# Last block of two chained MLPs: three subtractions on another engine, the two accumulators stored in the other order, stores issued by two queues

## The chip, the cores and the metric

The kernel runs on one core of one Trainium2 chip. The metric is the device time of one execution in microseconds (us); the median of several runs is what counts. The engines are TensorE (PE, matrix products; its weight loads are PEld), VectorE (DVE), ScalarE (ACT), GpSimd (POOL) and SyncE (SP, which here only issues DMAs). In lists of waits, PEq, ACTq and SPq are the instruction queues of engines.

## The reference

Only what matters is kept. A causal convolution over 7 positions with one set of softmax weights for each of 8 groups of channels gives 16384 tokens of 192 channels; two MLPs with 2048 hidden channels follow one another.

```python
def _attn_ref(x, weight):            # x: 4 x 4096 x 192, weight: 8 x 7
    w = softmax(weight, axis=-1)
    ...
    out = np.einsum('hk,bskhg->bshg', w, x_unf)     # 7 shifted copies of x
    return out.reshape(B, S, D).astype(np.float32)

def _moe_ref(x, w_in, w_out):        # w_in: 192 x 2048, w_out: 2048 x 192
    h = x @ w_in
    g = h * np.cos(h)
    return (g @ w_out).astype(np.float32)

def _moe2_ref(x, w_in, w_out):
    h = x @ w_in
    g = np.where(h > 0.0, h, np.exp(np.minimum(h, 0.0)) - 1.0)
    return (g @ w_out).astype(np.float32)
```

## The kernel before

The tokens are cut into 32 blocks of 512, kept with the channels on the partitions. Each hidden layer is cut into 16 pieces of 128 channels, so that one step is (m, b, f): MLP m (1 or 2), block b, piece f. There are 1024 steps in the list `steps` (m = 1 and m = 2 alternate by groups of four blocks), and `total` is their number. The last sixteen steps are MLP 2 of block 31, the last block.

Products are made of numbers split in a high and a low part (`gh` and `gl`, `wo_h` and `wo_l`), both in the type fp32r, so that a sum of several products keeps nearly the precision of float32. Of one step s, `emit_A` makes five products of 512 columns into the PSUM tile `u` (L474). ACT and DVE work out the activation into `w` (for MLP 2: L484, L501 on ACT, then L509 on DVE). `emit_hi` rounds `w` to `gh` on ACT (L515), and `emit_lo` makes the low part `gl = w - gh` on POOL (L520). `emit_B` adds five products to the block's two accumulators `a[0]` and `a[1]` (L531 to L535): three with `gh`, two with `gl`. `a[0]` holds the output channels 0 to 127. `a[1]` holds the last 64 channels in two halves of its partitions, which still have to be added.

`step(s)` sets the order: A of step s, then `emit_act2` and `emit_g` of step s-1, `emit_hi` and `emit_lo` of step s-2 (HID = 2) and B of step s-5 (LAG = 5). So when the last A is done, six Bs are left for PE: those of the steps total-6 to total-1. There are three buffers for `gh` and two for `gl` (`bufs=3`, `bufs=2`): a `gl` may be written only when the B two steps earlier has read its buffer.

After B of a block's last piece, `evac` empties the accumulators. For m = 1 it makes the four tiles that MLP 2 reads (L544 to L549). For m = 2 it queues the generator `store(b, a)`: ACT copies the upper half of `a[1]` (L563), DVE transposes `a[0]` in blocks of 32 x 32 (L565), SP issues four stores of 32 channels each, 64 KB (L560); then DVE adds the two halves of `a[1]` (L568) and transposes the sum (L571), and SP issues two more stores. For block 31 all of this comes after the last product.

The order of all instructions on an engine is the order of the code, with one exception. The first 108 steps (`for s in range(FREE)`) stand outside `tc.manual_schedule()`: there a scheduler at build time orders the instructions of each engine by its own estimates of times. In these steps DVE, ACT and POOL also split the weights of both MLPs (the function `decode`, L176 to L184, works on pieces of `raw`), and DVE applies the convolution (L355, L357).

Of the kernel before, what the change touches and what calls it, by code (L numbers as in the profile page):

```python
# [9 lines left out]
F32 = mybir.dt.float32  # L10
# [4 lines left out]
ALU = mybir.AluOpType  # L15
AX = mybir.AxisListType

P = 128
N = 512
Q = 32  # L20
# [16 lines left out]
def conv_then_two_mlps(ctx, tc, x, weight, w_in1, w_out1, w_in2, w_out2, out):  # L37
# [9 lines left out]
    nc = tc.nc  # L47
# [8 lines left out]
    D2 = D - P  # L56
    HALO = K - 1
    NBLK = T // N
# [7 lines left out]
    op = ctx.enter_context(tc.tile_pool(name="op", bufs=1))  # L66
# [10 lines left out]
    f32 = lambda ap: ap.bitcast(F32)  # L77
# [3 lines left out]
    oseg = out.rearrange("(i j) d -> i j d", j=J)  # L81
# [381 lines left out]
    wrk = {}  # L463
# [47 lines left out]
    gs = {}  # L511
# [5 lines left out]

    def emit_lo(s):
        gl = wk.tile([P, N], F32R, tag="gl", name="gl", bufs=2)
        nc.gpsimd.tensor_tensor(out=gl, in0=wrk.pop(s), in1=f32(gs[s][0]), op=ALU.subtract)  # L520
        gs[s].append(gl)

    def emit_B(s):
        m, b, f = steps[s]
        gh, gl = gs.pop(s)
        st, sp = f == 0, f == NF - 1
        if f == 0:
            acc[m, b] = [ps_a.tile([P, N], F32, tag="acc", name="acc") for _ in range(2)]
        a = acc[m, b]
        h, l, sel = (wo[m, n] for n in ("h", "l", "s"))  # L530
        nc.tensor.matmul(a[0], lhsT=l[:, f, :], rhs=gh, start=st, stop=False)  # L531
        nc.tensor.matmul(a[0], lhsT=h[:, f, :], rhs=gh, start=False, stop=False)  # L532
        nc.tensor.matmul(a[1], lhsT=sel[:, f, :], rhs=gh, start=st, stop=False)  # L533
        nc.tensor.matmul(a[0], lhsT=h[:, f, :], rhs=gl, start=False, stop=sp)  # L534
        nc.tensor.matmul(a[1], lhsT=sel[:, f, :], rhs=gl, start=False, stop=sp)  # L535
        if f == NF - 1:
            evac(m, b)

    def evac(m, b):
        a = acc.pop((m, b))  # L540
        if m == 1:
            xh, xl, x3, x4 = (zt.tile([P, N], F32R, tag=n, name=n) for n in ("zh", "zl", "z3", "z4"))
            al = op.tile([P, N], F32R, tag="al", name="al")[0:D2]
            nc.scalar.activation(out=xh, in_=a[0], func=AF.Copy, scale=TWO_PI)  # L544
            nc.scalar.activation(out=x4, in_=a[1], func=AF.Copy, scale=TWO_PI)
            nc.vector.scalar_tensor_tensor(out=xl, in0=a[0], scalar=TWO_PI, in1=f32(xh), op0=ALU.mult, op1=ALU.subtract)
            nc.vector.scalar_tensor_tensor(out=al, in0=a[1][0:D2], scalar=TWO_PI, in1=f32(x4[0:D2]), op0=ALU.mult, op1=ALU.subtract)
            nc.sync.dma_start(out=f32(x3[0:D2]), in_=f32(x4[0:D2]))
            nc.sync.dma_start(out=f32(x3[D2:P]), in_=f32(al))  # L549
            xs[2, b] = (xh, xl, x3, x4)  # L550
        else:
            chores.append(store(b, a))

    def store(b, a):
        cols = lambda ap: ap.rearrange("p (j i) -> p j i", i=Q)
        j = slice(b * JB, (b + 1) * JB)

        def put(o, ch0, n):
            for ch in range(0, n, Q):
                nc.sync.dma_start(out=oseg[:, j, ch0 + ch:ch0 + ch + Q], in_=cols(o[ch:ch + Q]))  # L560

        lower = op.tile([P, N], F32, tag="al", name="lower")[0:D2]
        nc.scalar.activation(out=lower, in_=a[1][D2:P], func=AF.Copy)  # L563
        o = op.tile([P, N], F32, tag="o1", name="o")
        nc.vector.transpose(out=o, in_=a[0])  # L565
        put(o, 0, P)
        yield
        nc.vector.tensor_tensor(out=lower, in0=a[1][0:D2], in1=lower, op=ALU.add)  # L568
        yield
        o = op.tile([P, N], F32, tag="o2", name="o")  # L570
        nc.vector.transpose(out=o[0:D2], in_=lower)  # L571
        put(o, P, D2)
        yield
# [102 lines left out]
    def emit_B2(s):  # L676
        need("out", steps[s][0], steps[s][2])
        emit_B(s)

    def step(s):  # L680
# [21 lines left out]
        if 0 <= s - HID < total:  # L702
            emit_lo(s - HID)
# [14 lines left out]
    total = len(steps)  # L718
# [56 lines left out]
```

## Time and profile before

| | us |
|---|---|
| median of 3 runs | 2382.76 |
| lowest and highest of these | 2382.19, 2385.02 |
| the profiled execution, its own time | 2383.45 |
| its span, first to last instruction | 2381.7 |
| PE busy in the span | 2357.3 (99%) |
| ACT, DVE, POOL busy | 1890.7, 1548.2, 1414.3 |

The span is read from the trace, and the execution's own time lies 1.75 us above it. A busy PE is the sum over overlapping products; the trace shows a product of 512 columns as 0.39 us long, while one starts every 0.227 us. A share of busy time says little about the two ends of the program, where an engine that is idle on average can be what everything waits for.

### The profile page before, as it was taken

To read this page: it belongs to the slowest core of one execution; us is meant where nothing else is said; L and a number is where in the kernel's file an instruction comes from. 1 tells how busy PE (TensorE), PEld (TensorE's weight loads), DVE (VectorE), ACT (ScalarE), POOL (GpSimd) and SP (SyncE) were. 2 spreads that over 40 slices of the span, in tenths; PEclk is the share of its full clock that TensorE was granted. 3 is DMA by queue.
4 is the path that set the end of the run, shared out by engine and by line. 5 is a ranking of instruction groups with operands and counts; after the bars stand their busy time and mean duration, and the time that the engine had idled before them with its cause. 6 is when DMAs were issued, how large, how long until landed. Compare 5 with 4: busy or idle time off the path is not lost.

```text
span 2381.7 us, 32340 instructions
## 1 busy us (share of the span) xinstructions
PE 2357.3 (99%) x10354; PEld 1936.5 (81%) x10354; DVE 1548.2 (65%) x2292; ACT 1890.7 (79%) x3378; POOL 1414.3 (59%) x1144
## 2 busy tenths in 40 slices
PE   8899999999999999999999999999999999999998
PEld 5678888888888888888888888888888888888887
DVE  6997569943699337983379733896349963497433
ACT  7888787787877878777787878778787787877876
POOL 6888655555555555555555555555555555555555
PEclk9999999999999999999999999999999999999999
DMA  6123111100111002110011001110011100110000
GB/s 167 47 71 81 26 24 28 30 10 10 29 29 25 12 7 34 27 22 12 14 28 37 16 7 17 26 37 16 7 20 33 26 16 14 18 19 16 5 14 14
DMA packets 251116, 65.05 MB, mean 27 GB/s; under 512 B 226112, under 2 KB 239424, under 8 KB 250944
## 3 DMA queue, kind: packets, MB, share of 16 engines
q1 hardware_dynamic: 250496, 62.59, 13.8%
q8 instruction: 81, 1.33, 0.2%
q14 instruction: 91, 0.75, 0.1%
q10 hardware_dynamic: 448, 0.39, 0.1%
HBM read 29.91 MB, written 12.58 MB: 18 GB/s over the span
## 4 chain that ended last, share of the span: by engine, by line
PE 95%; DVE 3%; ACT 1%; DMA 1%; issue 0%; ACTq 0%; SPq 0%; POOL 0%; DVEq 0%
PE u L474 47%; PE acc L531 9%; PE acc L533 9%; PE acc L532 9%; PE acc L534 9%; PE acc L535 9%; DVE y L357 1%; DVE w L493 1%; DVE w L507 1%; PE y L400 0%; DMA early<-in_moe_w_in_dram 0%; DVE w L181 0%; DVE early L182 0%; DVE t L180 0%; ACT w L482 0%
## 5 line engine op out<-in xcount | busy, mean ns | idle before, releaser
L520 POOL TENSOR_TENSOR gl<-w,gh 128x512 fp32r<-128x512 f32 x1024 | 1336.6, 1306 | 928.2 <-PE acc L535 595.8
L509 DVE SCALAR_TENSOR_TENSOR w<-w,u 128x512 f32<-128x512 f32 x512 | 351.7, 687 | 675.1 <-ACT w L501 654.6
L515 ACT ACTIVATE gh<-w 128x512 fp32r<-128x512 f32 x1024 | 643.7, 629 | 20.8 <-DVE w L507 8.3
L499 ACT ACTIVATE w<-w 128x512 f32<-128x512 f32 x512 | 323.1, 631 | 203.6 <-DVE w L493 199.5
L484 ACT ACTIVATE w<-u 128x512 f32<-128x512 f32 x512 | 306.6, 599 | 211.9 <-PE u L474 208.3
L474 PE MATMUL u<-xh,wi_hl 128*128 128x512 f32 x1024 | 399.4, 392 | 12.9 <-DVE w L507 6.5
L507 DVE TENSOR_TENSOR w<-u,w 128x512 f32<-128x512 f32 x512 | 348.9, 682 | 88.1 <-ACT w L499 83.5
L531 PE MATMUL acc<-gh,wo_l 128*128 128x512 f32 x1024 | 399.6, 390 | 1.9 <-ACT gh L515 1.9
L534 PE MATMUL acc<-gl,wo_h 128*128 128x512 f32 x1024 | 399.6, 390 | 0.8 <-POOL gl L520 0.6
L535 PE MATMUL acc<-gl,wo_s 128*128 128x512 f32 x1024 | 398.4, 389 | 0.0
L533 PE MATMUL acc<-gh,wo_s 128*128 128x512 f32 x1024 | 398.4, 389 | 0.0
L532 PE MATMUL acc<-gh,wo_h 128*128 128x512 f32 x1024 | 398.4, 389 | 0.0
L474 PE MATMUL u<-zh,wi_hl 128*128 128x512 f32 x1024 | 397.7, 389 | 0.0
L493 DVE SCALAR_TENSOR_TENSOR w<-u,w 128x512 f32<-128x512 f32 x512 | 347.6, 679 | 10.8 <-ACT w L482 9.4
L501 ACT ACTIVATE w<-w 128x512 f32<-128x512 f32 x512 | 317.0, 619 | 0.6
L482 ACT ACTIVATE w<-u 128x512 int32<-128x512 f32 x512 | 299.2, 585 | 22.2 <-PE u L474 19.2
L474 PE MATMUL u<-x,wi_s 128*128 128x512 f32 x1024 | 315.8, 390 | 0.0
L474 PE MATMUL u<-z,wi_s 128*128 128x512 f32 x1024 | 315.2, 389 | 0.0
L357 DVE SCALAR_TENSOR_TENSOR y<-xT,wch,y 128x512 f32<-128x512 f32 x276 | 297.5, 1078 | 0.2
L474 PEld LDWEIGHTS u<-xh,wi_hl 128*128 128x128 f32 x1024 | 192.5, 188 | 59.3 <-DVE w L507 10.8
L531 PEld LDWEIGHTS acc<-gh,wo_l 128*128 128x128 f32 x1024 | 192.2, 188 | 43.6 <-ACT gh L515 3.4
L534 PEld LDWEIGHTS acc<-gl,wo_h 128*128 128x128 f32 x1024 | 192.1, 188 | 43.7 <-POOL gl L520 4.1
(94 smaller groups left out, 2352.8 us busy)
## 6 DMA issues: line engine op xcount, KB each, us to landing
out_dram<-o SPq DMA_DIRECT2D x192, 64.0 KB, 2.0
xa<-in_x_dram SPq DMA_DIRECT2D x112, 88.0 KB, 3.0
xc<-in_x_dram SPq DMA_DIRECT2D x56, 88.0 KB, 3.0
z<-z SPq DMA_DIRECT2D x32, 128.0 KB, 2.3
z<-al SPq DMA_DIRECT2D x32, 128.0 KB, 2.2
x<-ch SPq DMA_DIRECT2D x30, 128.0 KB, 2.2
x<-cl SPq DMA_DIRECT2D x30, 128.0 KB, 2.3
early<-in_moe_w_out_dram SPq DMA_DIRECT2D x12, 256.0 KB, 4.3
```

Of the source, the lines that this page charges most:

```text
L474: led[0] = nc.tensor.matmul(u, lhsT=wi[m, w][:, c], rhs=xx, start=i == 0, stop=i == len(ops) - 1).ins
L493: paced[0] = nc.vector.scalar_tensor_tensor(out=w, in0=u, scalar=0.25, in1=w.bitcast(I32), op0=ALU.add, op1=ALU.subtract).ins
L499: nc.scalar.activation(out=w, in_=w, func=AF.Sin, scale=6.283185)
L507: nc.vector.tensor_tensor(out=w, in0=u, in1=w, op=ALU.mult)
L509: paced[0] = nc.vector.scalar_tensor_tensor(out=w, in0=w, scalar=-1.0, in1=u, op0=ALU.add, op1=ALU.max).ins
L515: nc.scalar.activation(out=gh, in_=wrk[s], func=AF.Copy)
L520: nc.gpsimd.tensor_tensor(out=gl, in0=wrk.pop(s), in1=f32(gs[s][0]), op=ALU.subtract)
L531: nc.tensor.matmul(a[0], lhsT=l[:, f, :], rhs=gh, start=st, stop=False)
L532: nc.tensor.matmul(a[0], lhsT=h[:, f, :], rhs=gh, start=False, stop=False)
L533: nc.tensor.matmul(a[1], lhsT=sel[:, f, :], rhs=gh, start=st, stop=False)
L534: nc.tensor.matmul(a[0], lhsT=h[:, f, :], rhs=gl, start=False, stop=sp)
L535: nc.tensor.matmul(a[1], lhsT=sel[:, f, :], rhs=gl, start=False, stop=sp)
```

## The change

In the last three steps (total-3, total-2, total-1) the subtraction of `emit_lo` runs on DVE in place of POOL. In `emit_B`, in all steps, the product of `gl` with `wo_s` into `a[1]` comes ahead of the product of `gl` with `wo_h` into `a[0]`, so that `a[1]` is finished first. For the last block alone, `store` adds and transposes `a[1]` first, issues its two stores, and only then transposes `a[0]` and issues four. Of these six stores SP issues three and ACT three.

```diff
     def emit_lo(s):
         gl = wk.tile([P, N], F32R, tag="gl", name="gl", bufs=2)
-        nc.gpsimd.tensor_tensor(out=gl, in0=wrk.pop(s), in1=f32(gs[s][0]), op=ALU.subtract)
+
+        engine = nc.vector if s >= total - 3 else nc.gpsimd
+        engine.tensor_tensor(out=gl, in0=wrk.pop(s), in1=f32(gs[s][0]), op=ALU.subtract)
         gs[s].append(gl)
...
         nc.tensor.matmul(a[1], lhsT=sel[:, f, :], rhs=gh, start=st, stop=False)
+        nc.tensor.matmul(a[1], lhsT=sel[:, f, :], rhs=gl, start=False, stop=sp)
         nc.tensor.matmul(a[0], lhsT=h[:, f, :], rhs=gl, start=False, stop=sp)
-        nc.tensor.matmul(a[1], lhsT=sel[:, f, :], rhs=gl, start=False, stop=sp)
         if f == NF - 1:
             evac(m, b)
...
         def put(o, ch0, n):
             for ch in range(0, n, Q):
-                nc.sync.dma_start(out=oseg[:, j, ch0 + ch:ch0 + ch + Q], in_=cols(o[ch:ch + Q]))
-
+
+                queue = nc.scalar if b == NBLK - 1 and ch // Q % 2 else nc.sync
+                queue.dma_start(out=oseg[:, j, ch0 + ch:ch0 + ch + Q], in_=cols(o[ch:ch + Q]))
+
+        last = b == NBLK - 1
         lower = op.tile([P, N], F32, tag="al", name="lower")[0:D2]
         nc.scalar.activation(out=lower, in_=a[1][D2:P], func=AF.Copy)
+        if last:
+
+            nc.vector.tensor_tensor(out=lower, in0=a[1][0:D2], in1=lower, op=ALU.add)
+            o2 = op.tile([P, N], F32, tag="o2", name="o")
+            nc.vector.transpose(out=o2[0:D2], in_=lower)
+            put(o2, P, D2)
         o = op.tile([P, N], F32, tag="o1", name="o")
         nc.vector.transpose(out=o, in_=a[0])
         put(o, 0, P)
+        if last:
+            return
         yield
```

With it the lines move: in the new code POOL's subtraction is L522, the five products of B are L533 to L537, the stores are issued at L564, and the last block's chain is L568, L571, L573, L576.

DVE at the end of the program, before. The rows begin in the store of block 30; L509 is the activation of a step of MLP 2.

```order
L565 STREAM_TRANSPOSE o<-acc 128x512
L509 SCALAR_TENSOR_TENSOR w<-w,u 128x512
L568 TENSOR_TENSOR lower<-acc,lower 64x512
L509 SCALAR_TENSOR_TENSOR w<-w,u 128x512
L571 STREAM_TRANSPOSE o<-lower 64x512
L509 SCALAR_TENSOR_TENSOR w<-w,u 128x512 x10
L565 STREAM_TRANSPOSE o<-acc 128x512
L568 TENSOR_TENSOR lower<-acc,lower 64x512
L571 STREAM_TRANSPOSE o<-lower 64x512
```

DVE at the same place, after:

```order
L509 SCALAR_TENSOR_TENSOR w<-w,u 128x512 x9
L522 TENSOR_TENSOR gl<-w,gh 128x512
L509 SCALAR_TENSOR_TENSOR w<-w,u 128x512
L522 TENSOR_TENSOR gl<-w,gh 128x512 x2
L571 TENSOR_TENSOR lower<-acc,lower 64x512
L573 STREAM_TRANSPOSE o<-lower 64x512
L576 STREAM_TRANSPOSE o<-acc 128x512
```

One subtraction now stands ahead of the last activation (L509 of step total-1), two behind it, and the transposition of `a[0]` has gone from the first to the last place of the final three.

ACT at the end of the program, after; before, the rows were the same up to the copy `lower<-acc` (L563), and that was the last.

```order
L484 ACTIVATE w<-u 128x512
L515 ACTIVATE gh<-w 128x512
L501 ACTIVATE w<-w 128x512
L515 ACTIVATE gh<-w 128x512 x2
L568 ACTIVATE lower<-acc 64x512
L564 DMA out_dram<-o 32x16x32 x3
```

ACT now issues three stores behind its copy, and SP's last row of stores has 21 in place of 24.

DVE in the first 108 steps, where the scheduler puts the order together: the piece of the difference around the second block's hand-over from MLP 1 to MLP 2. L546 and L547 before (L548 and L549 after) empty the accumulators, L507 and L493 belong to activations of MLP 1, L178 to L182 split weights, L445 splits a block of input.

```order
-L546 SCALAR_TENSOR_TENSOR zl<-acc,zh 128x512
-L547 SCALAR_TENSOR_TENSOR al<-acc,z_1365 64x512
-L507 TENSOR_TENSOR w<-u,w 128x512
-L445 TENSOR_TENSOR xl<-y,xh 128x512
-L178 TENSOR_SCALAR t<-raw 128x256
+L549 SCALAR_TENSOR_TENSOR al<-acc,z_1365 64x512
+L548 SCALAR_TENSOR_TENSOR zl<-acc,zh 128x512
+L507 TENSOR_TENSOR w<-u,w 128x512
+L445 TENSOR_TENSOR xl<-y,xh 128x512
 L493 SCALAR_TENSOR_TENSOR w<-u,w 128x512 x2
```

The two that empty the accumulators have changed places, since `a[1]` is now finished first, and from here on the splitting of weights is dealt out differently among the activations. Ahead of the first such swap the order of DVE, ACT and POOL is what it was; with the last of the 108 steps the difference ends.

## Rows read from the trace of the kernel before

**Rows 1.** Busy time by stretch (us from the start), PEclk is the granted clock:

```profile
core 0: us, PE busy (x) PEld busy (x) DVE busy (x) ACT busy (x) POOL busy (x), PEclk, DMA share, GB/s
10.00:20.00 10.00, 5.42 (x22) 2.55 (x22) 6.92 (x15) 5.00 (x15) 3.79 (x7) 1.00 1.09 303
60.00:110.00 50.00, 42.67 (x171) 30.16 (x170) 48.02 (x84) 39.42 (x84) 41.63 (x39) 1.00 0.17 40
110.00:130.00 20.00, 20.00 (x89) 16.17 (x88) 18.80 (x27) 16.21 (x31) 13.60 (x12) 1.00 0.21 49
130.00:140.00 10.00, 8.85 (x39) 6.79 (x38) 8.49 (x17) 7.81 (x17) 5.95 (x5) 1.00 0.26 78
140.00:160.00 20.00, 20.00 (x90) 16.52 (x89) 18.90 (x41) 18.22 (x39) 19.07 (x21) 1.00 0.33 86
160.00:2360.00 2200.00, 2200.00 (x9708) 1821.67 (x9707) 1408.15 (x2029) 1756.09 (x3094) 1286.76 (x1003) 1.00 0.12 22
```

**Rows 2.** Timeline of the end: start, duration, [idle before <- releaser]:

```profile
2369.37 5.05 POOL L520 TENSOR_TENSOR gl<-w,gh 128x512 fp32r<-128x512 f32 x4 [0.97 <-PE acc L535]
2370.04 0.69 DVE L509 SCALAR_TENSOR_TENSOR w<-w,u 128x512 f32<-128x512 f32 x1 [1.58 <-ACT w L501]
...
2371.32 0.40 PE L531 MATMUL acc<-gh,wo_l 128*128 128x512 f32 x1
2371.38 0.63 ACT L515 ACTIVATE gh<-w 128x512 fp32r<-128x512 f32 x1 [0.78 <-PE acc L533]
...
2371.98 0.19 PEld L534 LDWEIGHTS acc<-gl,wo_h 128*128 128x128 f32 x1 [0.24 <-POOL gl L520]
...
2373.23 0.19 PEld L534 LDWEIGHTS acc<-gl,wo_h 128*128 128x128 f32 x1 [0.26 <-POOL gl L520]
...
2374.47 0.19 PEld L534 LDWEIGHTS acc<-gl,wo_h 128*128 128x128 f32 x1 [0.25 <-POOL gl L520]
...
2374.82 0.39 PE L535 MATMUL acc<-gl,wo_s 128*128 128x512 f32 x1
2375.01 0.72 DVE L565 STREAM_TRANSPOSE o<-acc 128x512 f32<-128x512 f32 x1 [4.29 <-PE acc L534]
2375.24 0.59 ACT L563 ACTIVATE lower<-acc 64x512 f32<-64x512 f32 x1 [3.23 <-PE acc L535]
2375.76 3.04 SPq L560 DMA_DIRECT2D out_dram<-o  x6
2375.87 0.68 DVE L568 TENSOR_TENSOR lower<-acc,lower 64x512 f32<-64x512 f32 x1
2376.59 0.70 DVE L571 STREAM_TRANSPOSE o<-lower 64x512 f32<-64x512 f32 x1
```

**Rows 3.** Chain that ended last: five products without a wait, then the last three Bs:

```profile
2366.93 1.13 PE u L474 x5
...
2371.25 0.23 PE acc L535
2371.48 0.23 PE acc L531
...
2374.98 0.24 PE acc L535
2375.22 0.02 issue
```

**Rows 4.** The last six stores: durations of the issues, last issue, time to landing:

```profile
L560 SPq DMA_DIRECT2D out_dram<-o x6: 315/494/507, 2375.8 to 2378.3; - x6
DMA to landing us min/median/max: 1.8/2.0/2.0
2378.30 0.51 SPq L560 DMA_DIRECT2D out_dram<-o  x1
```

**Rows 5.** DMA engines from 2376.6 to 2379.95: busy tenths, then packets and share:

```profile
DMA  4899885799885899988579989568989757999961
q1 hardware_dynamic: 3167, 0.39, 80.8%
```

**Rows 6.** Two queues issuing side by side at the start of the program:

```profile
1.28 3.86 SPq L283 DMA_DIRECT2D rows<-in_x_dram  x4
0.82 1.19 ACTq L209 DMA_DIRECT2D early<-in_moe_w_in_dram  x2
2.05 1.28 ACTq L194 DMA_DIRECT2D early<-in_moe_w_in_dram  x2
```

**Rows 7.** A DVE subtraction of two SBUF tiles: ns min/median/max, 32 of them:

```profile
L445 DVE TENSOR_TENSOR xl<-y,xh x32: 671/1137/1458, 20.8 to 2177.2; 128x512 fp32r<-128x512 f32 x32
```

**Rows 8.** Groups of DVE by line and shape: busy us, mean ns:

```profile
L507 DVE TENSOR_TENSOR w<-u,w 128x512 f32<-128x512 f32 x512 | 348.9, 682 | 88.1 <-ACT w L499 83.5
L493 DVE SCALAR_TENSOR_TENSOR w<-u,w 128x512 f32<-128x512 f32 x512 | 347.6, 679 | 10.8 <-ACT w L482 9.4 <-POOL w L184 0.7
L180 DVE TENSOR_SCALAR t<-t 128x256 f32<-128x256 f32 x46 | 19.6, 427 | 9.8 <-ACT t L179 9.6
```

**Rows 9.** The chain that ended last, around 130 us:

```profile
128.94 1.46 DVE y L357
130.40 0.02 issue
130.42 3.16 DMA raw<-in_moe_w_out_dram
```

## The prediction

> **What bounds the kernel now.** I read the busy times by stretch first, then the end of the timeline, then the stores. From 160 to 2360 us PE is busy for all of 2200 us at a granted clock of 1.00, and the list of who waits for whom has nothing for PE in between [rows 1]. Nothing in that stretch gets shorter unless PE has fewer products, and the change removes none. What can move is the two ends: the first 140 us, where PE lost 7.33 us between 60 and 110 and 1.15 us between 130 and 140 [rows 1], and the end, from the last six Bs to the last instruction at 2381.7.
>
> The end before, event by event. POOL makes the last four `gl` back to back, 5.05 us for 4, that is 1.26 each [rows 2], while a B takes PE only 5 x 0.227 = 1.13. So each of the last three Bs waits a little for its `gl`: their weight loads stood idle 0.24, 0.26 and 0.25 us [rows 2]. On the chain, these three Bs run from 2371.48 to 2375.22, 3.74 us, where 15 products at 0.227 (1.13 for five) take 3.40 [rows 3]: 0.34 us lost. The last product ends at 2374.82 + 0.39 = 2375.21. DVE transposes `a[0]` from 2375.01 to 2375.73, and SP issues the first store at 2375.76; the sum of `a[1]` is transposed by 2376.59 + 0.70 = 2377.29 [rows 2]. SP takes 0.49 us an issue and starts one every (2378.30 - 2375.76) / 5 = 0.51 us; the last starts at 2378.30 and lands 2.0 later, at 2380.30 [rows 4]. Then 1.4 us pass to the end of the span. The chain of waits ends with the copy, the addition and the transposition of `a[1]`, but SP was still at the fourth store of `a[0]` when that result came: the queue was the later of the two, by half a microsecond.
>
> **The change, part by part.**
>
> *Three subtractions on DVE.* The trace has a DVE subtraction of the same form (two SBUF tiles, 128x512, fp32r out): 671 ns at the least and 1458 at the most [rows 7]. The long ones lie beside a POOL subtraction. In the new end POOL's last `gl` (step total-4) runs from 2369.37 to about 2370.67, and after that POOL is done. So I take 0.68 for each, from about 2370.67 on. The first (step total-3) waits for B of step total-5, whose products end near 2370.34, and for POOL; it runs to 2371.35. Behind it in DVE's queue stands the last activation, L509 of step total-1, which began at 2370.04 before [rows 2]; now it runs 2371.38 to 2372.07. The last rounding on ACT (0.63) follows, to 2372.75, in place of 2372.01. The second subtraction runs to 2372.76, the third to 2373.46. PE wants them at 2372.00, 2373.13 and 2374.26, and the last `gh` at 2373.58, all counted from the B at 2371.32 with 0.227 a product. The smallest margin is 0.37 us. So the wait of 0.34 goes, and the last product ends at 2374.88. Bounds: at 1458 ns for the first alone the second comes 0.13 late, and the saving shrinks to 0.2; that is the other end.
>
> *The swapped products.* Five products a step before and after, at the same 0.227. In the body of the program the only effect is that the emptying of `a[0]` may start 0.23 later and that of `a[1]` 0.23 earlier, under 2200 us of PE that waited for nobody [rows 1]: zero. If that cover were gone it would be 0.23 for each of 64 accumulations, 15 us; but DVE is idle for 36% of that stretch and ACT for 20%, and the inputs of MLP 2 are made three blocks ahead for most blocks, so I keep zero.
>
> *The new order of the last stores.* `a[1]` is finished at 2374.88 - 0.23 = 2374.65. Copy 0.59, addition 0.68, transposition 0.70, each about 0.03 behind the one before [rows 2]: 2376.74. There both queues issue one store. The transposition of `a[0]`, which was first before, now comes last: 0.72, to 2377.49. So the first store is issued at 2376.77 (before: 2375.76) and the last four can begin at 2377.52, on two queues. What they cost is unknown, since the trace never has stores on two queues. Three bounds:
> - If issuing was all that held the stores, two queues issue two at a time: the last starts at 2377.52 + 0.5 and lands 2.0 later, 2380.05, 0.25 earlier than before. That ACT can issue beside SP is seen at the start of the program: four on ACT in 2.5 us while SP issued its own [rows 6].
> - If the stores keep the pace of before, 3.35 us of data for six [rows 5], beginning 0.84 after the first issue as before: data from 2377.61 to 2380.96. Before, data ended 0.35 ahead of the last landing, so it lands at 2381.31: 1.0 later.
> - Between: the 16 DMA engines were busy 80.8% of those 3.35 us [rows 5], so one store costs 3.35 x 0.808 / 6 = 0.45 us of all of them. At full use six take 2.71, landing at 2380.67, 0.37 later. At the highest share that the trace shows, 1.09 [rows 1], they take 2.48, landing at 2380.44, 0.14 later.
>
> I take the middle of the last two, +0.25 us, because the engines at four fifths are nearer to full than the queue has room to gain.
>
> The Trainium skill, "DMA: Bandwidth & Descriptors", section "Issuing engines are not separate DMA queues", says that DMAs started by different engines run on the same 16 DMA engines and interleave, and that a second issuer saves only the time of initiating, usually small beside the transfer. By that rule alone the stores keep their pace and the change loses 1.0 us; rows 4 and 5 speak for part of it only, since here an issue of 0.49 us is as long as the spacing of the stores and the engines had a fifth of their time free.
>
> *The first 108 steps.* The code of the change touches them only by the swap, but the scheduler dealt out the rest anew from about 115 us on. Until then the order is the same, so the 7.33 us between 60 and 110 stay. After that PE lost 1.15 us, behind a load of weights that kept DVE waiting until 133.6 [rows 1, 9]: the most that can be gained. On the side of loss I counted, along DVE's two orders, the work that stands ahead of each activation, at 0.68 an activation and 0.41 to 0.43 a piece of weight work [rows 8]: no L493 or L507 has more than 1.9 us more ahead of it than before. DVE is busy 92% of 110 to 160 [rows 1], so such a delay could reach PE once. I take zero, between -1.15 and +1.9.
>
> **The sum.** The profiled execution took 2383.45. With +0.25 for the end (the saved 0.34 of PE is inside it) and 0 for the head that is 2383.7. The median of the three runs lies 0.69 below the profiled one, so against 2382.76 it is 2383.0. A measurement of this kernel can tell a change from none at about 0.2%, 4.8 us; the forecast is no change.
>
> **The rivals.**
> - *The stores keep one pace.* Two queues feed the same engines and nothing is won, while the first store starts 1.0 later: +1.0 us, 2383.8. For it: the engines were busy at 8 or 9 tenths in most slices [rows 5]. Against: the share was set by issues of 0.49 at a spacing of 0.51 [rows 4]. It is what the Trainium skill's section above has as a rule.
> - *Issuing was all, and the gap at 134 us closes.* -0.25 - 1.15 = -1.4, 2381.4. For it: ACT issued beside SP at the start [rows 6]. Against: only a fifth of the engines' time is free.
> - *The wait moves to DVE.* The first subtraction holds up the last activation, and the chain through it arrives after PE wants it. At 1458 ns each the first ends at 2371.86, the activation at 2372.58, the second at 2374.04 and the third at 2375.50, against 2374.26: 1.24 on top of the forecast, 2384.2. Against it: the long ones need POOL at work, and POOL is done.
> - *The head gets slower, and the kernel with it.* Between 60 and 110 us, where DVE was busy 48.02 of 50, PE lost 7.33 us [rows 1]. If the new order makes PE trail DVE in the same measure from 115 to 180, where weights for MLP 2 are split, it loses 65 x 7.33 / 50 = 9.5 us: 2392. It decides from a loss of 4.8. Against it: in that stretch the old order lost 1.15 with DVE just as full, and the new one shifts no activation by more than 1.9.
> - *Faster beyond the measurement.* The end has 0.34 of waits and about 3 us of copies and issues to give, the head 1.15. All of it together does not reach 4.8.
>
> **How the numbers follow.** Forecast (end within 0.4 either way, head unchanged): 0.62. One pace: 0.13. Issue-bound and the gap closed: 0.12. The wait on DVE: 0.05. Head slower by over 4.8: 0.06. Faster by over 4.8: 0.02. The first four are within 0.2%: 0.92. The likeliest is 2383.0. The range takes in -1.4 with the lowest run (0.57 below the median) at the low end, 2380.8, and at the high end +1.0 for the stores and +1.9 for the head with half a microsecond for the spread of runs, 2386.2. It leaves out most of the last two cases and about a tenth for runs like the highest one.
>
> **What would show it.** In the new profile no weight load of the last three Bs waits for a `gl`, and the three Bs take 3.40 us on the chain. The subtractions on DVE last 0.68. The first store is issued about 1.9 us after the last product, and the last landing lies between 5.2 and 6.4 us after it. DMA share over the stores is 0.9 to 1.1 (engines), about 0.8 (one pace). From 140 to 160 us PE is busy throughout. The prediction is wrong if PE has idle time beyond 140 us, or if a subtraction on DVE takes over a microsecond with POOL at rest.

## The result and the profile after

The changed kernel is slower: 2397.07 us, the median of 6 runs (2396.56 to 2398.02), against 2382.77 for the kernel before (6 runs, 2382.19 to 2385.02). The ratio is 1.0058, with an interval of 1.0048 to 1.0068. The forecast was 2383.0 with a range up to 2386.2, so the result lies 10.9 us outside. The spans of the two profiled executions, 2395.2 and 2381.7, differ by 13.5 us; that is what has to be found.

I read the busy time by stretch first, in the stretches of [rows 1] and with the long one cut up:

```profile
core 0: us, PE busy (x) PEld busy (x) DVE busy (x) ACT busy (x) POOL busy (x), PEclk, DMA share, GB/s
60.00:110.00 50.00, 42.69 (x171) 30.19 (x170) 48.05 (x85) 39.42 (x83) 41.72 (x39) 1.00 0.18 42
130.00:140.00 10.00, 9.64 (x42) 7.49 (x41) 9.59 (x20) 8.71 (x18) 6.03 (x6) 1.00 0.21 54
140.00:160.00 20.00, 20.00 (x90) 16.57 (x89) 19.16 (x41) 18.11 (x39) 19.44 (x22) 1.00 0.37 94
160.00:420.00 260.00, 260.00 (x1148) 215.39 (x1147) 190.16 (x301) 212.74 (x394) 171.19 (x146) 1.00 0.22 44
420.00:500.00 80.00, 79.27 (x344) 63.87 (x343) 68.32 (x91) 60.06 (x112) 44.27 (x34) 1.00 0.12 23
500.00:750.00 250.00, 250.00 (x1105) 207.10 (x1104) 161.60 (x222) 194.44 (x342) 142.62 (x110) 1.00 0.12 21
424.00:484.00 60.00, 59.27 (x256) 47.28 (x255) 56.47 (x73) 41.87 (x78) 32.33 (x26) 1.00 0.13 23
```

The head has not suffered: 42.69 us of PE between 60 and 110, as before, and 9.64 in place of 8.85 from 130 to 140. The granted clock is 1.00 throughout. But in the body, where PE had never waited, there is now a stretch in which it does. Products overlap, so the 0.73 us of idle time there understate the loss.

The place can be followed over the whole kernel by one instruction that comes once a block: `zh`, ACT's copy of `a[0]` at the hand-over from MLP 1 to MLP 2. Its starts, read from the timelines of the two kernels, in us:

| block | before | after | after minus before |
|---|---|---|---|
| 4 | 385.68 | 384.40 | -1.28 |
| 5 | 421.95 | 420.66 | -1.29 |
| 6 | 458.21 | 460.60 | +2.39 |
| 7 | 494.48 | 496.13 | +1.65 |
| 8 | 675.82 | 676.88 | +1.06 |
| 9 | 712.08 | 713.15 | +1.07 |
| 10 | 748.35 | 753.09 | +4.74 |
| 12 | 965.95 | 969.37 | +3.42 |
| 24 | 1836.35 | 1846.87 | +10.52 |
| 28 | 2126.48 | 2139.35 | +12.87 |
| 31 | 2235.28 | 2248.15 | +12.87 |

From one group of four blocks to the next (4 to 8, 24 to 28) the changed kernel loses 2.34 or 2.35 us: `zh` falls back by 3.7 at the group's third block and regains 1.3 in the next two. From block 4 to block 28 that happens six times, and in the last group not at all: there the last tap of the convolution starts at 2165.2, ahead of the second hand-over. So there are six equal losses in the body, 14.1 us; the head gains 1.3 to 1.5, and the end, below, loses 0.8.

PE's list of waits between 140 and 2370 us, empty before, names the two it waits for (us in total, times, longest):

```profile
engine line waited for: us in total, times, longest us
PE u L474 <- DVE w L507: 2.1, 9, 0.3
PE acc L536 <- POOL gl L522: 1.6, 6, 0.3
```

And one group of DVE's instructions has grown, the convolution's taps (busy us, then mean ns of one). Before:

```profile
L357 DVE SCALAR_TENSOR_TENSOR y<-xT,wch,y 128x512 f32<-128x512 f32 x276 | 297.5, 1078 | 0.2
```

After:

```profile
L357 DVE SCALAR_TENSOR_TENSOR y<-xT,wch,y 128x512 f32<-128x512 f32 x276 | 330.9, 1199 | 0.2
```

The same 276 taps take 33.4 us more. The change does not touch them. They are run in the steps of MLP 1, and where the loss lies DVE was nearly full already. The last row of the busy times above is for the 60 us in which the first loss comes about. The same row before:

```profile
424.00:484.00 60.00, 60.00 (x266) 49.69 (x265) 54.28 (x78) 46.77 (x85) 34.73 (x27) 1.00 0.14 26
```

DVE was busy for 54.28 of 60 us, not for the 64% that the average over 2200 us shows [rows 1], and is now busier with five instructions fewer. PE starts ten products fewer, 10 x 0.227 = 2.27 us of its work.

### Where the taps change

The timeline at the hand-over of block 5, before (start, duration, engine and line):

```profile
421.95 0.60 ACT L544 ACTIVATE zh<-acc 128x512 fp32r<-128x512 f32 x1
...
422.58 0.69 DVE L546 SCALAR_TENSOR_TENSOR zl<-acc,zh 128x512 fp32r<-128x512 f32 x1
...
423.78 0.67 DVE L493 SCALAR_TENSOR_TENSOR w<-u,w 128x512 f32<-128x512 f32 x1
...
424.38 0.73 DVE L357 SCALAR_TENSOR_TENSOR y<-xT,wch,y 128x512 f32<-128x512 f32 x1
...
424.64 1.64 POOL L520 TENSOR_TENSOR gl<-w,gh 128x512 fp32r<-128x512 f32 x1 [0.95 <-DVE w L493]
```

The same place after:

```profile
420.66 0.60 ACT L546 ACTIVATE zh<-acc 128x512 fp32r<-128x512 f32 x1
...
421.30 0.69 DVE L548 SCALAR_TENSOR_TENSOR zl<-acc,zh 128x512 fp32r<-128x512 f32 x1 [0.25 <-ACT zh L546]
...
422.50 0.67 DVE L493 SCALAR_TENSOR_TENSOR w<-u,w 128x512 f32<-128x512 f32 x1
...
423.10 1.86 DVE L357 SCALAR_TENSOR_TENSOR y<-xT,wch,y 128x512 f32<-128x512 f32 x1
...
423.13 1.29 POOL L522 TENSOR_TENSOR gl<-w,gh 128x512 fp32r<-128x512 f32 x1 [0.97 <-PE acc L537]
```

PE's beat is 1.51 us earlier here: the last product into an accumulator starts at 420.24 and started at 421.75. POOL's `gl` keeps to that beat, 423.13 against 424.64. `zh` does not. It reads `a[0]`, which is now finished by the last product of the five and no longer by the last but one, so it starts 0.42 us behind that product's start, where it started 0.20 behind. DVE waits 0.25 us for it, and `zl`, `al`, L493 and the tap all come later by 0.22 in the beat. Before, the tap started 0.26 ahead of POOL's `gl`, took 0.73, and POOL needed 1.64. Now it starts 0.03 ahead, POOL takes its usual 1.29, and the tap takes 1.86. So one of the two works and the other stands still, and 0.2 us decide which. It is the same at all six places of the loss, the hand-overs of blocks 5, 9, 13, 17, 21 and 25: 0.26 ahead and 0.73 before, 0.03 ahead and 1.86 or 1.87 after.

That one stands still can be read from every tap. From 160 us on each of the two traces has 252. A tap that starts while a `gl` is at work, or up to 0.03 ahead of it, ends at least 0.54 after that `gl` (199 taps before, 221 after). One that starts 0.25 or more ahead of the next `gl` takes 0.73 to 0.75 (53 and 31), and no tap lies in between. To start first by the trace is therefore not enough: a tap that is 0.03 ahead still waits.

The Trainium skill, "SBUF — State Buffer", section "Who interferes with whom", has this as a rule: a DVE instruction with two SBUF inputs contends with a GpSimd instruction that reads SBUF, under an exclusive lock. The trace agrees: 0.73 and 1.64 one way, 1.86 and 1.29 the other.

From there the taps fall into another pattern. Some of those that follow, after:

```profile
444.94 1.13 DVE L357 SCALAR_TENSOR_TENSOR y<-xT,wch,y 128x512 f32<-128x512 f32 x1
...
447.19 1.47 DVE L357 SCALAR_TENSOR_TENSOR y<-xT,wch,y 128x512 f32<-128x512 f32 x1
...
449.79 1.12 DVE L357 SCALAR_TENSOR_TENSOR y<-xT,wch,y 128x512 f32<-128x512 f32 x1
...
465.01 1.73 DVE L357 SCALAR_TENSOR_TENSOR y<-xT,wch,y 128x512 f32<-128x512 f32 x1
...
467.86 0.86 DVE L357 SCALAR_TENSOR_TENSOR y<-xT,wch,y 128x512 f32<-128x512 f32 x1
...
469.84 1.74 DVE L357 SCALAR_TENSOR_TENSOR y<-xT,wch,y 128x512 f32<-128x512 f32 x1
```

Before, they took 1.15 each from 445.74 to 454.81, one every 2.27 us, which is PE's ten products. Now two steps take 4.85 us (444.94 to 449.79) or 4.83 (465.01 to 469.84), where PE wants 20 x 0.227 = 4.54. DVE falls behind PE by 0.3 us in two steps until PE has to wait, first for a `gl` (at 463.66), then for DVE. A piece of the chain that ended last (start, duration) shows the second wait; in it DVE works without a gap:

```profile
461.83 0.67 DVE al L549
462.50 0.60 DVE w L493
463.10 0.80 DVE y L355
463.89 0.60 DVE w L507
464.49 0.60 DVE w L493
465.09 1.65 DVE y L357
466.74 0.61 DVE w L507
467.40 1.45 PE u L474 x5
```

### The end

The timeline of the end, which answers to [rows 2]:

```profile
2383.11 0.74 DVE L522 TENSOR_TENSOR gl<-w,gh 128x512 fp32r<-128x512 f32 x1 [2.01 <-PE acc L537]
...
2384.38 0.68 DVE L522 TENSOR_TENSOR gl<-w,gh 128x512 fp32r<-128x512 f32 x1
...
2385.35 0.69 DVE L522 TENSOR_TENSOR gl<-w,gh 128x512 fp32r<-128x512 f32 x1 [0.29 <-PE acc L537]
...
2387.12 0.39 PE L537 MATMUL acc<-gl,wo_h 128*128 128x512 f32 x1
2387.32 0.59 ACT L568 ACTIVATE lower<-acc 64x512 f32<-64x512 f32 x1 [2.12 <-PE acc L536]
2387.95 0.68 DVE L571 TENSOR_TENSOR lower<-acc,lower 64x512 f32<-64x512 f32 x1 [1.91 <-ACT lower L568]
2388.66 0.70 DVE L573 STREAM_TRANSPOSE o<-lower 64x512 f32<-64x512 f32 x1
2389.30 0.67 DVE L576 STREAM_TRANSPOSE o<-acc 128x512 f32<-128x512 f32 x1
2389.40 1.62 SPq L564 DMA_DIRECT2D out_dram<-o  x3
```

No weight load waits for a `gl` any more. Counted from the last product's end (2387.12 + 0.39 = 2387.51), the first store is issued 1.89 later and the last landing comes at 6.17; before it was 5.10. The stores, as in [rows 4] (durations of the issues in ns, first and last issue, time to landing):

```profile
L564 SPq DMA_DIRECT2D out_dram<-o x3: 315/316/658, 2389.4 to 2390.4; - x3
L564 ACTq DMA_DIRECT2D out_dram<-o x3: 376/380/706, 2389.4 to 2390.4; - x3
DMA to landing us min/median/max: 2.1/2.7/3.3
```

The two queues' shares of the DMA engines from 2390.2 to 2393.25, as in [rows 5]:

```profile
q10 hardware_dynamic: 1584, 0.20, 45.8%
q1 hardware_dynamic: 1584, 0.20, 44.3%
```

The data of the six stores take 2.99 us, 90% of the engines, where they took 3.35 at 80.8%. Issued closer together, each store lands later, 2.7 us (the median) after its issue in place of 2.0.

**The sum.** Head, by PE's beat at block 5: -1.51. Body: 6 x 2.35 = +14.1. The last fifteen products, first to last start and the last's end, 3.56 us in place of 3.89: -0.33. From the last product to the end of the span, 7.70 in place of 6.52: +1.18. Together +13.4, against 13.5 between the spans.

### The profile page after: what moved, and what is told of

It is laid out like the page before. It is cut to its first block, busy times and chain, and to the rows that moved or that the text cites. A ratio compares the mean times of both kernels' runs of the same rounds, so it can differ in the third digit from the quotient of the medians.

```text
span 2395.2 us, 32315 instructions
## 1 busy us (share of the span) xinstructions
PE 2366.0 (99%) x10354; PEld 1934.4 (81%) x10354; DVE 1584.5 (66%) x2295; ACT 1878.6 (78%) x3378; POOL 1406.5 (59%) x1141
## 4 chain that ended last, share of the span: by engine, by line
PE 92%; DVE 5%; ACT 1%; DMA 1%; issue 1%; POOL 0%; ACTq 0%; SPq 0%; DVEq 0%; POOLq 0%
PE u L474 46%; PE acc L534 9%; PE acc L533 9%; PE acc L535 9%; PE acc L536 9%; PE acc L537 9%; DVE y L357 2%; DVE w L493 1%; DVE w L507 1%; PE y L400 0%; DMA early<-in_moe_w_in_dram 0%; ACT w L482 0%; POOL gl L522 0%; DVE y L355 0%; DVE al L549 0%
## 5 line engine op out<-in xcount | busy, mean ns | idle before, releaser
L522 POOL TENSOR_TENSOR gl<-w,gh 128x512 fp32r<-128x512 f32 x1021 | 1329.1, 1302 | 948.5 <-PE acc L537 560.3
L509 DVE SCALAR_TENSOR_TENSOR w<-w,u 128x512 f32<-128x512 f32 x512 | 352.0, 688 | 656.5 <-ACT w L501 640.1
L507 DVE TENSOR_TENSOR w<-u,w 128x512 f32<-128x512 f32 x512 | 348.1, 681 | 85.6 <-ACT w L499 82.3
L533 PE MATMUL acc<-gh,wo_l 128*128 128x512 f32 x1024 | 399.9, 390 | 1.9 <-ACT gh L515 1.9
L537 PE MATMUL acc<-gl,wo_h 128*128 128x512 f32 x1024 | 398.8, 389 | 0.0
L493 DVE SCALAR_TENSOR_TENSOR w<-u,w 128x512 f32<-128x512 f32 x512 | 347.1, 678 | 8.4 <-ACT w L482 8.0
L357 DVE SCALAR_TENSOR_TENSOR y<-xT,wch,y 128x512 f32<-128x512 f32 x276 | 330.9, 1199 | 0.2
L536 PEld LDWEIGHTS acc<-gl,wo_s 128*128 128x128 f32 x1024 | 192.3, 188 | 47.0 <-POOL gl L522 7.4
L533 PEld LDWEIGHTS acc<-gh,wo_l 128*128 128x128 f32 x1024 | 192.3, 188 | 43.6 <-ACT gh L515 3.4
```

The source lines that it names most:

```text
L357: behind[0] = nc.vector.scalar_tensor_tensor(out=o, in0=i, scalar=w, in1=o, op0=ALU.mult, op1=ALU.add).ins
L493: paced[0] = nc.vector.scalar_tensor_tensor(out=w, in0=u, scalar=0.25, in1=w.bitcast(I32), op0=ALU.add, op1=ALU.subtract).ins
L507: nc.vector.tensor_tensor(out=w, in0=u, in1=w, op=ALU.mult)
L509: paced[0] = nc.vector.scalar_tensor_tensor(out=w, in0=w, scalar=-1.0, in1=u, op0=ALU.add, op1=ALU.max).ins
L522: engine.tensor_tensor(out=gl, in0=wrk.pop(s), in1=f32(gs[s][0]), op=ALU.subtract)
```

## The experiments

Three theories stood at the outset: the loss comes from the swap of the two products in the body; it comes from the head, which the scheduler orders anew with the swap; it comes from the end. Then, with the body found guilty, which instance of the swap does it, and by what.

**Everything but the swap.**

```diff
+        nc.tensor.matmul(a[0], lhsT=h[:, f, :], rhs=gl, start=False, stop=sp)
         nc.tensor.matmul(a[1], lhsT=sel[:, f, :], rhs=gl, start=False, stop=sp)
-        nc.tensor.matmul(a[0], lhsT=h[:, f, :], rhs=gl, start=False, stop=sp)
```

(against the changed kernel)

> The changed kernel with the two products of gl in their old order, everywhere; the three subtractions on DVE, the new order of the last stores and the two queues stay. Theory (the swapped products cost it all, away from the end): head and body as before, the end loses 1.18 us after the last product and gains the 0.34 of PE's waits, so about 0.8 over before: 2383.6 us, and no wait of PE between 140 and 2370. Rival (the edits of the last block cost it): about 2397.

Measured: 2384.53 (10 runs) against 2383.60 for the kernel before on the same chip, ratio 1.0004 (0.9995 to 1.0014). PE's list of waits from 140 to 2370 us is empty, and a tap takes 1079 ns. The last landing comes 6.39 us after the last product, 0.2 later than in the changed kernel, and the whole is 0.9 us above the kernel before: the end is not where 14 us went.

**Nothing but the swap**, on the kernel before.

```diff
+        nc.tensor.matmul(a[1], lhsT=sel[:, f, :], rhs=gl, start=False, stop=sp)
         nc.tensor.matmul(a[0], lhsT=h[:, f, :], rhs=gl, start=False, stop=sp)
-        nc.tensor.matmul(a[1], lhsT=sel[:, f, :], rhs=gl, start=False, stop=sp)
```

> The kernel before with the swapped products alone, in all steps. Theory: the head 1.5 earlier as in the changed kernel, then six losses of 2.35 us, 14.1 together: about 2395.3 us. Rival (the last block's edits): 2382.8 or 1.5 less.

Measured: 2396.73 (4 runs) against 2383.60, ratio 1.0055 (1.0040 to 1.0070). The taps take 1198 ns and PE has the two waits of the changed kernel. The swap is the whole loss, and the end is not.

**The swap at the hand-overs alone**: the last step of MLP 1 of each block, from step 108 on, 28 swaps out of 1024.

```diff
+        low = [(a[0], h), (a[1], sel)]
+        if s >= FREE and m == 1 and f == NF - 1:
+            low.reverse()
+        for o, w in low:
+            nc.tensor.matmul(o, lhsT=w[:, f, :], rhs=gl, start=False, stop=sp)
```

(in place of the two products)

> The kernel before with the products swapped only in the step that hands a block over from MLP 1 to MLP 2 (m = 1, last piece), and only behind the first 108 steps: 28 swaps in all. Theory (the copy of a[0] to zh starts 0.23 later there, DVE's work behind it too, and the next convolution tap then starts after POOL's subtraction instead of ahead of it): all of the loss, six times 2.35, with the head of before: about 2396.9 us. Rival (the other swaps shift something in each step): 2382.8.

**The swap in all other steps from 108 on.**

```diff
-        if s >= FREE and m == 1 and f == NF - 1:
+        if s >= FREE and not (m == 1 and f == NF - 1):
```

> The kernel before with the products swapped in every step behind the first 108 except those hand-over steps. Theory: 2382.8 us, no wait of PE between 140 and 2370, taps as long as before. Rival: about 2396.9.

Measured: the hand-overs alone 2397.87 (4 runs), ratio 1.0060 (1.0043 to 1.0077); all the others 2383.82 (10 runs), ratio 1.0001 (0.9991 to 1.0010), both against 2383.60. The taps of the first, and then of the second:

```profile
L357 DVE SCALAR_TENSOR_TENSOR y<-xT,wch,y 128x512 f32<-128x512 f32 x276 | 331.6, 1202 | 0.2
```

```profile
L357 DVE SCALAR_TENSOR_TENSOR y<-xT,wch,y 128x512 f32<-128x512 f32 x276 | 297.4, 1077 | 0.2
```

So 28 swapped pairs out of 1024, which change no work and no order on any engine but PE, cost 14 us. The order in the head is the old one in both kernels: the head is cleared.

**The late `zh` without the swap.** A copy on ACT of 0.41 us of constants, ahead of `zh` at the same 28 hand-overs, on the kernel before. The copy's result is not used.

```diff
+            if b >= GROUP:
+                late = op.tile([P, 2, P], F32, tag="late", name="late")
+                nc.scalar.activation(out=late, in_=f32(wo[m, "h"])[:, 0:2, :], func=AF.Copy)
             nc.scalar.activation(out=xh, in_=a[0], func=AF.Copy, scale=TWO_PI)
```

> The kernel before, products in their old order, with one ACT copy more (128x256, a constant into a tile that nobody reads) ahead of zh at the 28 hand-overs behind the first 108 steps. It makes zh start about 0.3 us later by another cause. Theory (only the start of DVE's work at the hand-over counts, since the next tap then starts behind POOL's subtraction): long taps and the six losses come back, near 2396.9 us. Rival (the products themselves, PE or the PSUM banks, do it): 2383.6, as before, since ACT is idle a fifth of the time.

Measured: 2400.05 (4 runs) against 2383.55, ratio 1.0069 (1.0054 to 1.0084), and the taps take 1202 ns. Its timeline at block 5:

```profile
422.22 0.41 ACT L546 ACTIVATE late<-wo_h 128x256 f32<-128x256 f32 x1
...
422.52 0.59 ACT L547 ACTIVATE zh<-acc 128x512 fp32r<-128x512 f32 x1
...
424.93 1.33 POOL L520 TENSOR_TENSOR gl<-w,gh 128x512 fp32r<-128x512 f32 x1 [0.97 <-PE acc L535]
424.95 1.86 DVE L357 SCALAR_TENSOR_TENSOR y<-xT,wch,y 128x512 f32<-128x512 f32 x1
```

`zh` stands 0.48 us behind the start of the last product (422.04), and the tap loses the race with the same 1.86. From block 4 to block 8 this kernel takes 292.86 us, where the kernel before takes 290.14 and the changed one 292.48. The products are in the old order, so it is the lateness that costs. Six times 2.72 is 16.3, more than the 14.1 of the swap and about 3 us more than was expected; `zh` is 0.28 later here, not 0.22, but why that costs more stays open.

**The swap, with no tap in the step of the hand-over.** The tap is run in a later step instead.

```diff
+        elif last and steps[s - LAG][0] == 1:
+            pass
         else:
             next(cq, None)
```

> The swapped products in all steps, but in the step of a hand-over (behind the first 108) no piece of convolution work is given to DVE; it comes one step later. No work is left out. Theory (the tap right behind the hand-over is the one that loses the race with POOL, and starts the slow pattern): no tap of 1.86 there and no wait of PE behind 140 us, 2382 us. Rival (the pattern starts from any tap, or from the delay in ACT's and PE's chain): 2390 to 2397.

**The swap, with `a[1]` emptied first at the hand-over**: ACT and DVE begin with the accumulator that is finished first.

```diff
+            if b >= GROUP:
+                nc.scalar.activation(out=x4, in_=a[1], func=AF.Copy, scale=TWO_PI)
+                nc.scalar.activation(out=xh, in_=a[0], func=AF.Copy, scale=TWO_PI)
+                nc.vector.scalar_tensor_tensor(out=al, ...)
+                nc.vector.scalar_tensor_tensor(out=xl, ...)
```

> The swapped products in all steps, and behind the first 108 the hand-over empties a[1] first too: ACT copies a[1] and then a[0], DVE works on a[1] and then on a[0]. DVE's first work then starts when it did before. Theory: DVE and POOL keep the phase of before, no wait of PE behind 140 us, 1.5 us less than before from the head: 2382 us. Rival (any change at the hand-over upsets it): about 2395 to 2397.

Measured: 2382.56 without the tap, ratio 0.9996 (0.9986 to 1.0006), and 2382.49 with the other order, ratio 0.9996 (0.9987 to 1.0006), 10 runs each against 2383.55. PE waits for nobody in the body of either. In the first, `zl` still waits 0.26 us for `zh`, but there is no tap for the delay to meet: the late copy alone costs nothing. In the second the tap of block 5 starts at 423.97 and takes 0.73, with `gl` at 424.22 taking 1.64, as in the kernel before. Both keep the swap in every step.

**The swap in the head alone** (`s < FREE`).

> The products swapped in the first 108 steps alone. Expected from the changed kernel's trace, whose steps run 1.51 us ahead of those before from 225 to 420 us: the same 1.5 here, to the end, so 2382.1 us against 2383.6, and a span of about 2380.2 to 2381. If the 1.5 came from the run and not from the order: no difference at 225 us.

Measured: one run, 2381.19 against 2383.55, with a span of 2379.5. `zh` of block 4 starts at 383.43, 2.25 earlier than before, so nearly the whole difference lies ahead of it; 1.5 was expected, and one run cannot tell how much of it is the order.

**Two queues, `a[0]` stored first as before.**

```diff
-                nc.sync.dma_start(out=oseg[:, j, ch0 + ch:ch0 + ch + Q], in_=cols(o[ch:ch + Q]))
+                queue = nc.scalar if b == NBLK - 1 and ch // Q % 2 else nc.sync
+                queue.dma_start(out=oseg[:, j, ch0 + ch:ch0 + ch + Q], in_=cols(o[ch:ch + Q]))
```

> The kernel before with the last block's stores issued by SP and ACT in turn, a[0] first as before. One pace (0.50 us a store whoever issues): the last landing 4.8 us after the last product, in place of 5.1. Issue-bound: 4.1, since the last two would start at 2377.3 and land 2.0 later. If the order of the stores and not the pace costs the changed kernel its end: also near 4.8, against 6.2 there.

Measured: one run, 2382.83 against 2383.26, which one run cannot tell apart. The trace can tell the end: the first store is issued 0.56 us after the last product, data run from 1.40 to 4.33, and the last landing comes at 4.78, against 5.10 before and 6.17 in the changed kernel. By these traces the second queue gains 0.3 us, and storing `a[1]` first costs 1.4.

**What is left over**: the swap in the head alone, the last three subtractions on DVE, two queues, `a[0]` first.

> What the runs so far left as a gain, together: products swapped in the first 108 steps alone, the three subtractions on DVE, two queues for the last block's stores, but a[0] stored first as before. From rows: head -1.5 (seen at 225 us in the kernel with that swap alone), PE's three waits -0.34; six stores that move at 0.50 us each on two queues (3.0 us of data for six in the kernel with old products and the new end) from the old first issue, instead of 0.56: -0.3. Together -2.1: 2381.4 us against 2383.55. If the stores gained what issuing allows: -0.8 in place of -0.3.

Measured: 2381.97 (11 runs, 2380.58 to 2382.68) against 2383.26 (15 runs), ratio 0.9994 (0.9985 to 1.0003). It is 15 us faster than the changed kernel. Against the kernel before it is 1.3 us lower, and the interval includes no change.

## Why the prediction was wrong

**The step that failed** is "The swapped products": "In the body of the program the only effect is that the emptying of `a[0]` may start 0.23 later", "so I keep zero". The effect itself was right, 0.22 later in the trace. Its price was not: 14.1 us. The cover was taken from an average, DVE idle for 36% of 2200 us and ACT for 20%. In the steps of MLP 1 that have taps DVE was busy 54.28 of 60, and its taps were shared with POOL by a race that a delay of 0.22 turns round. The step did name a price of 15 us "if that cover were gone", but for another mechanism, 0.23 at each of 64 accumulations. That the two sums are close is chance: the loss is 2.35 at each of six places. The rows for the right price were at hand: [rows 7] has another DVE instruction with two SBUF inputs at 671 and at 1458 ns, and the prediction put the long ones down to POOL, but asked only at the last three subtractions whether an instruction would come to lie beside one. Nor is it enough to lie beside one: the trace has seven of those instructions at 685 ns with a `gl` that starts 0.47 after them, and the long ones (1431 to 1458) start 0.38 to 0.41 after a `gl`. What counts is which of the two gets to work first.

**The rival that came nearest in size**, a slower head, was wrong in its place. Its loss of 7.33 between 60 and 110 stayed. From 130 to 140 PE lost 0.36 in place of 1.15, so the gap behind the load did close by 0.8. One `gl` of block 4, which started at 386.11 before and at 384.60 after, started at 385.69 to 386.87 in the six kernels with the old order in the head and at 383.85 to 385.69 in the six with the new. The bound of -1.15 for the head is near the difference of their means, 1.3, but the two sets touch: how much of it is the order and how much varies from run to run stays open.

**The three subtractions on DVE** went as predicted: 0.74, 0.68 and 0.69 us against 0.68 assumed, no wait of PE, and 0.33 saved against 0.34.

**The end.** The first store came 1.89 us after the last product, as forecast, and the last landing at 6.17, inside 5.2 to 6.4. But the forecast for the whole end was +0.25, and it is 1.18 - 0.33 = +0.85. The term mis-sized is the pace of the stores: 2.99 us for the six, where I took the mean of 2.71 and 2.48, 2.60. That is 0.4 of the 0.6 that are missing; the landing behind the data and the end behind the landing took 0.1 longer each. The rival of one pace (+1.0) was nearer than the forecast. The engines filled to 90% only, at the lower edge of the 0.9 to 1.1 that was to show them as the limit.

**The sign of being wrong** was named in advance: "if PE has idle time beyond 140 us".

What stays open: the trace shows the race turned at block 5 and PE waiting at block 6. Why the new pattern of taps, once begun, goes on by itself (1.13 and 1.47 in turn, then 1.73 and 0.86) was followed in the rows, but not tested for itself.

## What to carry to other kernels

Where the bound engine waits for nobody, ask of every delay not what the idle share is on average, but how full each engine is in the very steps that the delay falls into. Where DVE and POOL both read SBUF side by side, look up which of the two starts first and by how much: a lead of 0.26 us is an order that nobody wrote down, and moving anything ahead of it can lose it for many steps. When an accumulator is finished in another order, empty it in that order too.

## What the runs showed of the hardware

- At the six hand-overs, a tap that starts 0.25 or 0.26 us ahead of POOL's subtraction takes 0.73 or 0.74 and POOL 1.64 or 1.65. One that starts within 0.03 of it, on either side, takes 1.85 to 1.87 and POOL 1.29 to 1.34. Of the eleven kernels with a tap at that place seven show the one and four the other, each at all six. What happens between 0.03 and 0.25 ahead no trace shows.
- Two queues on the same six stores of 64 KB bring the data down from 3.35 to 2.99 us (2.94 with `a[0]` first), while the landing behind the issue goes up from 2.0 to 2.7 us (medians). The Trainium skill, "DMA: Bandwidth & Descriptors", section "Issuing engines are not separate DMA queues", says that a second issuer saves only the time of issuing; the trace agrees for the most part, 0.3 us at the end of the kernel.
